# A table of offsets on the priorities of a planned order (attention and a gated feed-forward block, one core)

## The chip, the core and the metric

The kernel runs on one core of a Trainium2 chip, as one program. Its time is the device time of an execution in microseconds; 0.2% of it is about 1.5 us. Before the change three executions took 748.99, 749.52 and 750.12 us. The core has five engines that work side by side, each through its own list of instructions in the order in which they stand there: TensorE (PE, with its weight loads as PEld), VectorE (DVE), ScalarE (ACT), GpSimd (POOL) and SyncE (SP), which issues the DMAs.

## The reference

Eight batch elements of 576 tokens, eight heads of 64 columns each, in fp32. The output of the attention is the input of the feed-forward block:

```python
scores = scale * np.matmul(q, k.transpose(0, 1, 3, 2))
cum = np.cumsum(np.maximum(s, 0.0), axis=-1)
bias = -(cum[:, :, :, None] - cum[:, :, None, :])
scores = np.where(causal, -1e9, scores + np.minimum(bias, 0.0))
attn = np.exp(scores - np.max(scores, axis=-1, keepdims=True))
attn = attn / (np.sum(attn, axis=-1, keepdims=True) + 1e-09)
x = heads_side_by_side(np.matmul(attn, v))            # 8 x 576 x 512
h = gelu_tanh(x @ w_in)                               # 512 -> 1024
u, v = h[..., :512], h[..., 512:]
v_n = (v - mean(v)) / np.sqrt(var(v) + 1e-6) * g_ln
v_s = np.einsum('ts,bsd->btd', w_sg, v_n) + b_sg[None, :, None]
return x + (u * v_s) @ w_out
```

## The kernel before, in words

The 64 pairs of batch element and head are called heads 0 to 63 here. For each head the scores are made in four products of up to 512 columns, in two PSUM banks in turn (pss). VectorE adds the mask and takes the row minimum (the scores are negated) while it copies them out (`p<-pss,mask`, with `mn`); ScalarE takes the exponential and its sum; GpSimd multiplies by the reciprocal of the sum in seven pieces (`p<-p,rs`); TensorE transposes the result in twelve blocks (`psp<-ident,p`); ScalarE and VectorE copy the transposes to SBUF (`pT<-psp`); and every second head TensorE multiplies the transposes of a pair of heads by their values (`psp<-pT,vf`), which gives 128 of the 512 columns of the block's input (`xr`). Heads 0 to 7 use fp32 products. From head 8 on, numbers are split into two parts of reduced precision ("hi" and "lo"): ScalarE or GpSimd makes hi, GpSimd the rest (`k<-raw,k`, `xs<-xr,xs`).

The feed-forward block of a batch element needs the split input of its four pairs of heads (xs). It is cut into units, each one PSUM bank (psm, three in turn): v-units 0 to 4 (128 tokens by 512 columns; gelu, then mean and variance on VectorE, six small steps `rt` on GpSimd, then the normalized value is split into `vn`), u-units (288 columns, gelu), s-units (the product with the spatial weights ws, times u, split into `gt`) and o-units (the product with w_out, plus x, stored). The order of the units is a list in the source (`ORDER`; `ORD0` for the first element). A unit's bank is free for a later unit when VectorE or ScalarE have read it for the last time.

At the start, heads 0 to 7 are made while the weights come in: eight parts of w_in and four of w_out are unpacked from 64 bit floats by ScalarE and VectorE (`psm<-pair`, `gt<-pair,psm`) and split by ScalarE and GpSimd (`wi<-gt`, `wo<-gt`), and the spatial weights are split too (`ws<-u`). Later elements overlap: while the block of one runs, the heads of the next are made.

What sets the order: the function that builds the kernel does not issue instructions, it records them as operations with their dependences (class `Plan`; all then have the line of `issue`, L293 before the change). `Plan.order` gives every operation a cost from a table in the source, and goes forward through the plan, at each moment giving an engine the available operation with the lowest priority number; then backward, to get for each operation the time by which it has to start, which is its priority in the next round. After five rounds the last forward pass is the order that `issue` writes out on every engine:

```python
        prio = list(range(len(ops)))
        rounds = ROUNDS if rounds is None else rounds
        for i in range(rounds):
            res = self.forward(lat, prio)
            if i < rounds - 1:
                prio = self.backward(lat, [t + o.busy for t, o in zip(self.start, ops)])
        if SHIFT:
            shift = np.frombuffer(zlib.decompress(base64.b85decode(SHIFT)), np.int8)
            res = self.forward(lat, [p + 200.0 * float(x) for p, x in zip(prio, shift)])
        return res
```

Before the change `SHIFT` is None and the last block is skipped.

Of the kernel before, what the change touches and what calls it, by code (L numbers as in the profile page):

```python
# [20 lines left out]
B, H, S, D = 8, 8, 576, 64  # L21
BH = B * H
DM, DFF = 512, 1024
DH = DFF // 2
P = 128
NC = DM // P
# [16 lines left out]
PO = [0, 64, 256, 640, 1152]  # L43
# [18 lines left out]
PROBE = None  # L62
ROUNDS = 5

SHIFT = None
N3 = 8
XR = 10
G = 2
# [23 lines left out]
class Plan:  # L92
# [73 lines left out]
    def order(self, lat=LAT, rounds=None):  # L166
# [13 lines left out]
# [7 lines that stand above are left out]
# [921 lines left out]
```

## Time and profile before

| | before |
|---|---|
| median of three executions | 749.52 us |
| the profiled execution, and its span | 749.63 us, 747.9 us |
| busy: PE, PEld | 728.8, 634.5 us |
| busy: POOL, ACT, DVE | 542.8, 473.3, 472.4 us |
| mean granted clock of TensorE | 0.991 |
| DMA queue of the loads and stores | 85.85 MB, 41.7% of 16 engines |

The span is the time from the first to the last instruction of the profiled execution; the execution's own time has 1.7 us around it. Busy time of TensorE is the union of its matmuls, whose ends are modelled. [...] A wait is idle time of an engine, put down to what ended it.

### The profile page before, as it was taken

Reading aid. Unit: us, or ns where it says so; the run is one execution under the profiler, and the core shown is the slowest. Engines: PE = TensorE matmul, PEld = TensorE weight load, DVE = VectorE, ACT = ScalarE, POOL = GpSimd, SP = SyncE. Lnnn points to the kernel's source line nnn. Section 1 sums busy time; section 2 is a strip of 40 time slices with the busy share of each in tenths; the row PEclk is TensorE's granted clock in tenths of the full one; section 3 lists DMA queues with packets and bytes.
Section 4 is the critical chain, followed back from the end, with each engine's and each line's share of the span. In section 5 each row is a group of like instructions: output and inputs, shape, how many; then the busy total and the mean of one; then the engine's idle time right before and its main releaser. Section 6 shows DMA issues by size and latency. Waiting matters only on the chain.

```text
span 747.9 us, 15982 instructions
## 1 busy us (share of the span) xinstructions
PE 728.8 (97%) x5219; PEld 634.5 (85%) x5219; DVE 472.4 (63%) x1470; ACT 473.3 (63%) x1279; POOL 542.8 (73%) x978
## 2 busy tenths in 40 slices
PE   8899889999999999999999999999999999999998
PEld 5666678988889898998889888899888988998998
DVE  7997668447664676646685376745766466843752
ACT  4898778457675677646785476755776457842440
POOL 4799999768679487866878676795868768674541
PEclk9999889999999999999999999999999999999999
DMA  6777544245444254343543543443543434300101
GB/s 215 211 224 185 150 113 125 86 110 139 117 125 121 77 160 121 94 133 99 148 125 86 143 123 112 125 109 90 155 123 88 141 98 133 82 8 32 47 8 64
DMA packets 59239, 86.87 MB, mean 116 GB/s; under 512 B 16482, under 2 KB 34148, under 8 KB 59156
## 3 DMA queue, kind: packets, MB, share of 16 engines
q1 hardware_dynamic: 59156, 85.85, 41.7%
q8 instruction: 41, 0.67, 0.4%
q14 instruction: 42, 0.34, 0.2%
HBM read 39.89 MB, written 9.73 MB: 66 GB/s over the span
## 4 chain that ended last, share of the span: by engine, by line
PE 87%; DVE 6%; POOL 2%; DMA 2%; issue 1%; ACT 1%; SPq 1%; POOLq 0%; DVEq 0%
PE psm L293 53%; PE psp L293 20%; PE pss L293 13%; DVE p L293 2%; DVE psm L293 2%; DMA pair<-in_w_in 1%; POOL p L293 1%; POOL xs L293 1%; DVE u L293 1%; POOL k L293 1%; SPq L293 1%; DVE gt L293 0%; DVE vt L293 0%; DMA k<-xs 0%; DVE pT L293 0%
## 5 line engine op out<-in xcount | busy, mean ns | idle before, releaser
L293 POOL TENSOR_SCALAR p<-p,rs 128x448 f32<-128x448 f32 x434 | 192.5, 452 | 26.0 <-DVE rs L293 8.9
L293 ACT ACTIVATE p<-p,mn 128x448 f32<-128x448 f32 x310 | 171.8, 556 | 49.6 <-DVE mn L293 49.2
L293 DVE CUSTOM_DVE_ANT_0 p<-pss,mask 128x448 f32<-128x448 f32 x310 | 122.0, 422 | 63.9 <-PE pss L293 55.1
L293 PE MATMUL pss<-k,q 128*128 128x288 f32 (+10 forms) x768 | 148.2, 311 | 6.2 <-DVE mn L293 5.7
L293 PEld LDWEIGHTS pss<-k,q 128*128 128x128 f32 (+3 forms) x768 | 120.7, 184 | 24.1 <-DVE mn L293 9.0
L293 PE MATMUL psm<-xs,wi 128*128 128x288 f32 x720 | 114.7, 303 | 2.8 <-DVE u L293 2.3
L293 PE MATMUL psm<-gt,wo 128*128 128x288 f32 x720 | 117.1, 301 | 0.0
L293 PE MATMUL psm<-ws,vn 128*128 128x288 f32 x708 | 112.3, 297 | 0.0
L293 PE MATMUL psm<-wi,xs 128*128 128x512 f32 (+1 forms) x380 | 105.5, 405 | 1.2 <-DVE vt L293 0.8
L293 PEld LDWEIGHTS psm<-xs,wi 128*128 128x128 f32 x720 | 100.6, 191 | 5.5 <-DVE u L293 3.7
L293 PEld LDWEIGHTS psm<-gt,wo 128*128 128x128 f32 x720 | 101.1, 188 | 1.9
L293 POOL TENSOR_TENSOR k<-raw,k 128x576 fp32r<-128x576 f32 x56 | 79.7, 1424 | 29.7 <-ACT k L293 28.5
L293 PEld LDWEIGHTS psm<-ws,vn 128*128 128x128 f32 x708 | 99.3, 188 | 0.4
L293 PE MATMUL psp<-pT,vf 128*64 128x64 f32 (+4 forms) x768 | 94.1, 393 | 0.2 <-ACT pT L293 0.2
L293 POOL TENSOR_TENSOR gt<-u,gt 128x288 fp32r<-128x288 f32 (+1 forms) x66 | 52.8, 804 | 51.4 <-ACT gt L293 51.4
L293 PEld LDWEIGHTS psp<-pT,vf 128*64 128x64 f32 x768 | 47.6, 137 | 49.0 <-issue 35.4
L293 ACT COPY pT<-psp 128x512 f32<-128x512 f32 x128 | 70.4, 579 | 20.0 <-PE psp L293 18.8
L293 PEld LDWEIGHTS psm<-wi,xs 128*128 128x128 f32 (+1 forms) x380 | 67.3, 187 | 14.8 <-DVE vt L293 1.1
L293 PEld LDWEIGHTS psp<-ident,p 128*128 128x128 f32 x744 | 69.7, 141 | 6.0 <-POOL p L293 4.2
L293 PE MATMUL psp<-ident,p 128*128 128x128 f32 x744 | 72.1, 248 | 2.8 <-POOL p L293 2.8
L293 ACT CAST gt<-u 128x288 fp32r<-128x288 f32 (+1 forms) x66 | 28.1, 429 | 61.8 <-DVE u L293 59.3
L293 DVE SCALAR_TENSOR_TENSOR u<-u,psm 128x288 f32<-128x288 f32 x120 | 52.4, 444 | 13.5 <-ACT u L293 12.4
(124 smaller groups left out, 1040.2 us busy)
## 6 DMA issues: line engine op xcount, KB each, us to landing
q<-k SPq DMA_DIRECT2D x168, 144.0 KB
raw<-in_kq SPq DMA_DIRECT2D x56, 288.0 KB
vf<-in_vp SPq DMA_DIRECT2D x64, 192.0 KB
out_t<-u SPq DMA_DIRECT2D x64, 144.0 KB
k<-k SPq DMA_DIRECT2D x56, 144.0 KB
pair<-in_w_in SPq DMA_DIRECT2D x8, 512.0 KB
pair<-in_w_out SPq DMA_DIRECT2D x4, 512.0 KB
u<-xs SPq DMA_DIRECT2D x32, 64.0 KB
```

The lines of the kernel that those rows point to most:

```text
L293: fn(*args, **kw)
```

## The change

One constant of the source changes; the code that reads it was there before, and all other lines stay:

```diff
-SHIFT = None
+SHIFT = (
+    'c-mc<^;;C*AND1rJ48YnDQOXrMoN$nkP!R`h)A=*0`n)Fh3$n68g}XKmhNt(yCkGR1fKQzUe7Pj>zA2pu9<7jobx{S`@UyKx)Fd<E@i$yPbjB6MY;Lf+1G'
+    '!rdkc2^d>(>?l!9;E{e(KUXJ>lt%_OwU4`p}@4fv15e_J-{+{duoU5RM~PrbOF(}c{#Mf|3&z8u7AF$KrfG%;~?_2mp^^dI!wH0S)Ba9?wq9xD@{>{sQm`'
...
+)
```

Unpacked, the text is 6,828 whole numbers from -120 to 120, one for each recorded operation; all but 18 are not zero. 200 times its number is added to an operation's priority, up to 24,000 of the plan's nanoseconds either way, and one more forward pass makes the order from these priorities. Operations, tiles and buffers are as before, so names agree between the two; the lines of the recorded instructions are 71 further down (L364). All five engines' lists come out in another order. TensorE's has 2,553 rows of equal neighbours before and 2,667 now. Three places follow, all between the first heads and the start of the first feed-forward block.

GpSimd, where the split of the fourth pair's input (xs_97, from heads 6 and 7) is made. Before; rs_92 is head 8's normalization, k2_117 the key split of head 11, ws_4 the spatial weights:

```order
L293 TENSOR_TENSOR ws_4_70<-u2_120_189,ws_4_70 128x288
L293 TENSOR_SCALAR p_0_66<-p_0_66,rs_92_161 128x448
L293 TENSOR_SCALAR p_0_66<-p_0_66,rs_92_161 64x64
L293 TENSOR_SCALAR p_0_66<-p_0_66,rs_92_161 128x320
L293 TENSOR_SCALAR p_0_66<-p_0_66,rs_92_161 128x128
L293 TENSOR_SCALAR p_0_66<-p_0_66,rs_92_161 64x64
L293 TENSOR_SCALAR p_0_66<-p_0_66,rs_92_161 128x512
L293 TENSOR_SCALAR p_0_66<-p_0_66,rs_92_161 64x64
L293 TENSOR_TENSOR ws_4_70<-u2_127_196,ws_4_70 128x288
L293 TENSOR_SCALAR xs_97_166<-xr_93_162 128x576
L293 TENSOR_TENSOR k2_117_186<-raw_110_179,k1_116_185 128x576
L293 TENSOR_TENSOR xs_97_166<-xr_93_162,xs_97_166 128x576
```

Now:

```order
L364 TENSOR_TENSOR k2_100_169<-raw_91_160,k1_99_168 128x576
L364 TENSOR_SCALAR p_0_66<-p_0_66,rs_92_161 128x448
L364 TENSOR_SCALAR p_0_66<-p_0_66,rs_92_161 128x320
L364 TENSOR_SCALAR p_0_66<-p_0_66,rs_92_161 64x64
L364 TENSOR_SCALAR xs_97_166<-xr_93_162 128x576
L364 TENSOR_TENSOR ws_4_70<-u2_127_196,ws_4_70 128x288
L364 TENSOR_TENSOR xs_97_166<-xr_93_162,xs_97_166 128x576
L364 TENSOR_TENSOR wr2_33_102<-u2_139_208,wr1_32_101 64x288
L364 TENSOR_TENSOR ws_4_70<-u2_114_183,ws_4_70 128x288
L364 TENSOR_TENSOR ws_4_70<-u2_115_184,ws_4_70 128x288
L364 TENSOR_SCALAR p_0_66<-p_0_66,rs_92_161 128x512
L364 TENSOR_SCALAR p_0_66<-p_0_66,rs_92_161 64x64
```

Four pieces of head 8's normalization, the key split and two splits of spatial weights (the two had been in front of the first row shown) now stand behind the second instruction of xs_97.

TensorE, at the transposes of head 9 (ident, p_3) and the start of v-unit 3 (psm1 from xs_79, xs_82, xs_90 and xs_97). Before; k1_116 is the key of head 11:

```order
L293 MATMUL psp2_62<-ident_16_85,p_3_69 128x128 x4
L293 MATMUL psp0_60<-ident_16_85,p_3_69 128x128 x4
L293 MATMUL psp1_61<-ident_16_85,p_3_69 128x128 x4
L293 MATMUL pss0_58<-k1_116_185,q1_118_187 128x448
L293 MATMUL pss0_58<-k2_117_186,q2_1_27_96 128x448
L293 MATMUL pss0_58<-k1_116_185,q1_118_187 64x64
L293 MATMUL pss0_58<-k2_117_186,q2_1_27_96 64x64
L293 MATMUL pss1_59<-k1_116_185,q1_118_187 128x320
L293 MATMUL pss1_59<-k2_117_186,q2_1_27_96 128x320
L293 MATMUL pss1_59<-k1_116_185,q1_118_187 128x192
L293 MATMUL pss1_59<-k2_117_186,q2_1_27_96 128x192
L293 MATMUL psm1_64<-wi_30_99,xs_79_148 128x512 x3
```

Now; k1_99 is the key of head 10, and u2_157 begins v-unit 4:

```order
L364 MATMUL psm0_63<-wi_30_99,xs_97_166 128x512
L364 MATMUL psm1_64<-wi_30_99,xs_79_148 128x512 x3
L364 MATMUL psm1_64<-wi_30_99,xs_82_151 128x512 x3
L364 MATMUL psm1_64<-wi_30_99,xs_90_159 128x512 x3
L364 MATMUL pss1_59<-k1_99_168,q1_101_170 128x288
L364 MATMUL pss1_59<-k2_100_169,q2_0_25_94 128x288
L364 MATMUL psm1_64<-wi_30_99,xs_97_166 128x512 x2
L364 MATMUL pss0_58<-k1_99_168,q1_101_170 128x288
L364 MATMUL pss0_58<-k2_100_169,q2_0_25_94 128x288
L364 MATMUL psm1_64<-wi_30_99,xs_97_166 128x512
L364 MATMUL psm2_65<-wi_30_99,u2_157_226 128x512
L364 MATMUL psp2_62<-ident_16_85,p_3_69 128x128 x4
```

All twelve matmuls of v-unit 3 and the first of v-unit 4 now stand ahead of the transposes of head 9; before, the transposes and the first scores of head 11 stood ahead of v-unit 3.

VectorE, around the reductions of v-unit 0 (vt_122 in bank psm1, bs_123, mv_124). Before; rs_111 is head 9's reciprocal, mn_119 head 10's scores, vt_134 and bs_135 are v-unit 1:

```order
L293 RECIPROCAL rs_111_180<-rs_111_180 128x5
L293 ISA p_0_66,mn_119_188<-pss0_58,mask_17_86 128x448
...
L293 ISA p_0_66,mn_119_188<-pss0_58,mask2_18_87 128x288
...
L293 SCALAR_TENSOR_TENSOR vt_122_191<-vt_122_191,psm1_64 128x512
L293 SCALAR_TENSOR_TENSOR vt_134_203<-vt_134_203,psm2_65 128x512
L293 ISA p_0_66,mn_119_188<-pss1_59,mask2_18_87,mn_119_188 128x288
...
L293 SCALAR_TENSOR_TENSOR psm1_64<-vt_122_191,psm1_64 128x512
L293 SCALAR_TENSOR_TENSOR psm2_65<-vt_134_203,psm2_65 128x512
L293 BN_STATS bs_123_192<-psm1_64 128x6
L293 BN_STATS bs_135_204<-psm2_65 128x6
L293 BN_AGGR mv_124_193<-bs_123_192 128x2
...
L293 SCALAR_TENSOR_TENSOR vt_122_191<-psm1_64,mv_124_193,g_b_20_89 128x512
```

Now; mn_104 is head 9's scores:

```order
L364 ISA p_2_68,mn_104_173<-pss0_58,mask2_18_87 128x288
...
L364 SCALAR_TENSOR_TENSOR vt_122_191<-vt_122_191,psm1_64 128x512
L364 ISA p_2_68,mn_104_173<-pss1_59,mask2_18_87,mn_104_173 128x288
...
L364 SCALAR_TENSOR_TENSOR psm1_64<-vt_122_191,psm1_64 128x512
L364 BN_STATS bs_123_192<-psm1_64 128x6
L364 SCALAR_TENSOR_TENSOR vt_134_203<-vt_134_203,psm2_65 128x512
L364 BN_AGGR mv_124_193<-bs_123_192 128x2
L364 RECIPROCAL rs_111_180<-rs_111_180 128x5
L364 SCALAR_TENSOR_TENSOR vt_122_191<-psm1_64,mv_124_193,g_b_20_89 128x512
L364 ISA p_0_66,mn_119_188<-pss0_58,mask_17_86 128x448
```

V-unit 0 gets its mean and variance (BN_AGGR) ahead of the reciprocal of head 9 and of all of head 10's scores, which stood ahead of it or between its steps.

## Rows read from the trace of the kernel before

**Rows 1.** The page's part 1: busy time, share of the span and instructions of each engine.

```profile
PE 728.8 (97%) x5219; PEld 634.5 (85%) x5219; DVE 472.4 (63%) x1470; ACT 473.3 (63%) x1279; POOL 542.8 (73%) x978
```

**Rows 2.** Windows: us, busy us of PE, PEld, DVE, ACT, POOL; PEclk, DMA share, GB/s.

```profile
10.00:62.00 52.00, 46.41 (x272) 31.50 (x271) 49.75 (x154) 45.85 (x133) 40.37 (x66) 1.00 0.73 220
62.00:80.00 18.00, 16.72 (x106) 12.32 (x107) 10.51 (x39) 13.60 (x38) 17.12 (x26) 1.00 0.69 163
80.00:104.00 24.00, 18.94 (x102) 14.15 (x101) 15.40 (x52) 18.66 (x51) 22.58 (x45) 0.80 0.51 136
104.00:145.00 41.00, 41.00 (x314) 37.45 (x314) 27.63 (x91) 29.72 (x83) 37.87 (x65) 0.95 0.41 111
145.00:640.00 495.00, 493.30 (x3656) 435.95 (x3655) 307.75 (x987) 319.42 (x868) 367.91 (x667) 1.00 0.44 119
720.00:748.00 28.00, 24.62 (x186) 24.38 (x184) 8.21 (x19) 3.84 (x10) 6.28 (x8) 1.00 0.14 48
```

**Rows 3.** Windows of the two stretches at a lower granted clock.

```profile
84.30:91.20 6.90, 6.05 (x20) 4.80 (x17) 4.65 (x17) 4.42 (x16) 6.90 (x15) 0.51 0.67 182
101.40:108.30 6.90, 6.03 (x28) 5.49 (x29) 5.67 (x17) 4.48 (x12) 6.44 (x16) 0.51 0.38 98
```

**Rows 4.** Waits of TensorE: us in total, times, longest.

```profile
PE pss L293 <- DVE mn L293: 5.7, 8, 1.5
...
PE psp L293 <- POOL p L293: 2.8, 2, 1.8
...
PE psm L293 <- DVE u L293: 2.3, 6, 0.6
...
PE pss L293 <- DMA k<-cum: 0.4, 1, 0.4
```

**Rows 5.** Timeline of TensorE from 70 to 110 us: start, length, instructions, idle before.

```profile
76.32 1.66 PE L293 MATMUL psm<-wi,xs 128*128 128x512 f32 x6 [0.18 <-POOL xs L293]
...
82.81 1.23 PE L293 MATMUL psp<-ident,p 128*128 128x128 f32 x12 [1.81 <-POOL p L293]
...
86.65 3.78 PE L293 MATMUL psm<-wi,xs 128*128 128x512 f32 x8 [0.85 <-DVE vt L293]
...
100.50 0.53 PE L293 MATMUL pss<-k,q 128*128 128x288 f32 x2 [1.16 <-DVE mn L293]
...
101.78 0.85 PE L293 MATMUL pss<-k,q 128*128 128x288 f32 x2 [0.75 <-DVE mn L293]
...
103.11 3.25 PE L293 MATMUL psm<-xs,wi 128*128 128x288 f32 x12 [0.48 <-DVE vt L293]
```

**Rows 6.** Groups of GpSimd's instructions by shape: count, busy us, mean ns.

```profile
L293 POOL TENSOR_TENSOR k<-raw,k 128x576 fp32r<-128x576 f32 x56 | 79.7, 1424 | 29.7 <-ACT k L293 28.5 <-DVE mn L293 1.2
...
L293 POOL TENSOR_SCALAR p<-p,rs 64x64 f32<-64x64 f32 x186 | 58.4, 314 | 10.3
...
L293 POOL TENSOR_SCALAR p<-p,rs 128x512 f32<-128x512 f32 x62 | 42.9, 693 | 5.4
...
L293 POOL TENSOR_SCALAR p<-p,rs 128x128 f32<-128x128 f32 x62 | 22.6, 365 | 0.0
...
L293 POOL TENSOR_TENSOR rt<-rt 128x1 f32<-128x1 f32 x96 | 18.4, 192 | 5.1
...
L293 POOL TENSOR_TENSOR rt<-rt,half 128x1 f32<-128x1 f32 x32 | 18.1, 565 | 1.9
...
L293 POOL TENSOR_TENSOR ws<-u,ws 128x288 fp32r<-128x288 f32 x8 | 6.3, 800 | 0.0
```

**Rows 7.** Timeline of GpSimd from 66 to 84 us.

```profile
77.97 1.42 POOL L293 TENSOR_TENSOR xs<-xr,xs 128x576 fp32r<-128x576 f32 x1
...
79.37 3.38 POOL L293 TENSOR_SCALAR p<-p,rs 128x448 f32<-128x448 f32 x7
```

**Rows 8.** Timeline of TensorE in two batches: the wait that recurs.

```profile
211.08 1.86 PE L293 MATMUL psm<-xs,wi 128*128 128x288 f32 x12 [0.43 <-DVE u L293]
...
298.67 1.58 PE L293 MATMUL psm<-xs,wi 128*128 128x288 f32 x10 [0.32 <-DVE u L293]
```

69 lines of the change are left out of this document (added).

## The prediction

> **What bounds the kernel now.** I read the busy times first. TensorE is busy for 97% of the span, the others for 63 to 73% [rows 1], so an order can only save what TensorE loses. The stretches say where that is [rows 2]: idle is 5.59 us from 10 to 62, 1.28 from 62 to 80, 5.06 from 80 to 104, nothing to 145, 1.70 in the 495 us from 145 to 640, and 3.38 in the last 28, of 19.1 in all (747.9 less 728.8 [rows 1]). The regular part, over 60% of the time, loses 0.3%: the question is settled in the first 104 us. There the cover is the other way round: from 10 to 62 VectorE is busy for 49.75 of 52 us, from 62 to 104 GpSimd for 39.7 of 42.
>
> [...]
>
> The waits themselves come last [rows 4, 5]. At 82.81 the transposes of head 9 wait for GpSimd's normalization; at 86.65 v-unit 3 waits for the bank that v-unit 0 holds until VectorE has read it; at 100.50 and 101.78 the scores of head 12 wait for the reductions that free their banks; at 103.11 u-unit 0 waits for the bank of v-unit 2.
>
> **The change part by part.** Nothing is removed or added: equal instructions, equal durations. TensorE's list goes from 2,553 to 2,667 rows of equal neighbours, so units are interleaved more finely; each instruction keeps its cost. I sum the moves by stretch.
>
> First, the fourth pair's split on GpSimd. It ends at 79.39 [rows 7] and all v-units need it. Seven instructions that stood ahead of it now stand behind: two splits of the spatial weights (0.80 each), one key split (1.42), and the last four pieces of head 8's normalization (0.69, 0.37 and twice 0.31), together 1.60 + 1.42 + 1.68 = 4.7 us [rows 6]. GpSimd has next to no idle time there, so work ahead is time: the split could end near 74.7. VectorE must not lose this lead again: v-unit 0's reductions now stand ahead of head 10's scores and of head 9's reciprocal, where before they stood behind and among them.
>
> Second, what pays for it. Ahead of the big piece of head 9's normalization now stand two splits of 0.80 and v-unit 0's six small steps (one power 0.57, five of about 0.19 [rows 6]): 1.60 + 0.57 + 0.95 = 3.1 us later, from 82.75 [rows 7] to about 86. TensorE's transposes of that head are behind v-unit 3 now, whose twelve matmuls fill up to 12 x 1.66/6 = 3.3 us [rows 5]. So the wait for head 9 is covered by the unit that waited for a bank before, if that bank comes as early as the first step says.
>
> The gain of the two together is at least 4.7 - 3.1 = 1.6 us, lead less lag, and at most the idle time of 80 to 104, 5.1 us. A loss is left to the rival below. I take 3.0, nearer the lower end, since head 9's normalization is what TensorE may still wait for.
>
> Third, the clock. Its two ends are a gain of 6.0 (both slow stretches gone) and a loss of 3.0 (a third one, if waits fall together elsewhere). With roughly half of the idle time gone I take one stretch gone: 3.0.
>
> Fourth, 10 to 62 us. The steps that unpack the weights (eight for the input, four for the output matrix) go behind score reductions on VectorE. VectorE's idle time there is 2.25 us, so the gain is at most that; a loss of the same size could come from unpacked weights that are late. I take 0: nearly all of these steps stay in that stretch. SP's moves belong here: the first weight load now goes out behind two others, and the key loads come up to a few places later or earlier. The nearest price is the one wait of TensorE for a DMA, 0.4 us [rows 4], and behind each of these loads stand other loads; I take 0, with 0.4 as the end on either side.
>
> Fifth, 145 to 640. The order is different in every round, but TensorE's work is the same. The gain is at most the 1.70 us of idle time; the loss has no bound but the second rival's. I take 0: engines other than TensorE have idle time of a quarter (GpSimd 368 of 495) to a third, which hides a move of some us. If that cover fails, each uncovered wait costs its 0.4 to 0.7 us (2.3 over 6 and 5.7 over 8 [rows 4]).
>
> Sixth, the end. The last 3.38 us are mostly the last addition and store, which nothing in the order shortens; the closing output units are still matmuls alone. 0.
>
> Sum: 3.0 + 3.0 = 6.0 us. The profiled execution took 749.63 us (747.9 of span and 1.7 around it), 0.1 over the median 749.52; 749.6 - 6.0 is 743.6.
>
> [...] From 145 to 640 the idle time is 1.70 us and the granted clock 1.00 throughout [rows 2]; short waits there cost nothing more. [...]
>
> **Rivals.** (a) More goes than I take: all idle time from 62 to 104 and both slow stretches: 749.6 - 6.3 - 6.0 = 737.3, and with the 1.7 of the regular part 735.6. For it speaks that the waits lie on one chain (split, v-unit, bank, next unit); against it that head 9 comes later.
>
> (b) Slower: new waits in the regular part. Each engine works its list in order. Where GpSimd or VectorE now reaches an instruction whose input isn't there, everything behind it is held, the next head's pieces too, and TensorE, with three banks for the units, has nothing else. The part has 495/87.6 = 5.65 rounds of eight heads (one batch of the input takes 298.67 - 211.08 = 87.6 us, from one wait for VectorE to its like [rows 8]). Two waits of 0.71 us a round are 8.0 us; if the clock falls in two of the rounds, 6.0 more. 749.6 - 6.0 + 8.0 + 6.0 = 757.6. It decides from about 1.1 us of new waits a round, against 0.30 now (1.70/5.65). Against it: GpSimd and VectorE have a quarter or more to spare; for it: the finer interleaving, and GpSimd's norm pieces with statistics steps between them. [...]
>
> (c) No change: head 9's pieces now stand alternately with v-unit 0's statistics steps on GpSimd. If VectorE delivers the statistics late, GpSimd stands and the lead of 4.7 is spent there: idle moves from the bank to the transposes, the clock falls as before. 749.6 - 0 = 749.6.
>
> That the table does nothing is excluded: all five engines' lists differ.
>
> **How the numbers follow.** The forecast, 737 to 748, gets 0.58, with 743.6 as its time; rival (a), under 737, 0.13; (c) 0.11; (b) 0.18. 0.2% is 1.5 us, about what a measurement of this kernel can tell from no change. Faster is the forecast and (a), 0.71; same is (c), 0.11; slower is (b), 0.18. The range leaves out a tenth at either end: 734 (1.6 under (a) with all) to 753, in the midst of (b). It is wide because one term, the clock, comes in steps of 3 us and the regular part has no upper bound.
>
> **What would show it.** Step one: the fourth pair's split ends 4 to 5 us earlier, v-unit 3 starts near 82 instead of 86.65. Step two: the transposes of head 9 wait less than 1.8 us, or not at all, behind v-unit 3. Step three: one stretch of half clock in the first 110 us instead of two. Step five: idle time of TensorE under 3 us from 145 to 640 and the clock at 1.00. The prediction is wrong if the idle time of 62 to 104 stays at 6.3, if both slow stretches stay, or if the regular part loses more than 7 us.

## The result

The time goes from 749.25 us (746.32 to 750.12) to 741.05 us (740.72 to 741.86), four executions each, a ratio of 0.9899 with a 95% interval of 0.9870 to 0.9927. A second comparison, with 15 executions of before, gave 741.09 and 0.9893 (0.9874 to 0.9912). The profiled execution of after took 741.86 us, its span is 740.1 (747.9 before): 7.8 us less.

Busy time of after, from the page's part 1 [rows 1]: TensorE has 6.0 us less, the others nearly the same.

```profile
PE 722.8 (98%) x5219; PEld 632.5 (85%) x5219; DVE 470.3 (64%) x1470; ACT 479.1 (65%) x1279; POOL 543.6 (73%) x978
```

Windows of after [rows 2]; the columns are those of before, and the last window ends 0.1 us ahead of the span's end:

```profile
10.00:62.00 52.00, 46.56 (x272) 31.45 (x270) 46.66 (x151) 44.69 (x129) 39.95 (x67) 1.00 0.73 209
62.00:80.00 18.00, 16.69 (x93) 12.88 (x94) 12.67 (x39) 14.79 (x39) 16.57 (x25) 0.91 0.64 177
80.00:104.00 24.00, 20.24 (x144) 16.11 (x143) 17.73 (x60) 20.68 (x57) 23.36 (x49) 1.00 0.55 143
104.00:145.00 41.00, 40.19 (x320) 36.05 (x319) 28.43 (x91) 31.23 (x86) 40.09 (x66) 1.00 0.47 122
145.00:640.00 495.00, 495.00 (x3678) 440.14 (x3677) 309.34 (x1001) 328.39 (x882) 370.91 (x672) 1.00 0.45 120
640.00:720.00 80.00, 80.00 (x577) 74.03 (x576) 43.28 (x101) 33.79 (x80) 42.86 (x81) 1.00 0.07 22
720.00:740.00 20.00, 16.91 (x128) 16.68 (x126) 6.13 (x14) 2.48 (x6) 3.96 (x5) 1.00 0.17 60
```

The same for the one window of before that was not shown:

```profile
640.00:720.00 80.00, 79.41 (x568) 72.48 (x567) 47.10 (x118) 39.48 (x96) 44.83 (x87) 1.00 0.10 30
```

TensorE's idle time from 62 to 104 us went from 6.34 to 5.07 us only, while it got through more: 144 matmuls instead of 102 from 80 to 104, at a granted clock of 1.00 instead of 0.80. From 145 to 720 us there is no idle time left, and 3,678 + 577 = 4,255 matmuls stand in the same 575 us that held 3,656 + 568 = 4,224: 31 more (22 by 640 us, 9 behind it), at 575/4,255 = 0.135 us each an estimated 4.2 us (3.0 and 1.2).

The granted clock, which the profile gives as a share of full speed: both half-clock stretches of before [rows 3] are gone, in the same windows it is 1.00. One of half the length is new, from 62.9 to 66.3 us:

```profile
62.90:66.30 3.40, 3.40 (x14) 2.71 (x13) 3.31 (x12) 3.27 (x11) 3.22 (x6) 0.50 0.90 243
84.30:91.20 6.90, 6.21 (x39) 4.28 (x39) 5.22 (x20) 6.30 (x19) 6.90 (x15) 1.00 0.53 135
101.40:108.30 6.90, 5.49 (x42) 5.13 (x43) 5.33 (x19) 5.79 (x15) 6.72 (x14) 1.00 0.42 100
```

TensorE's waits in after [rows 4]: the six for VectorE's u steps in the regular part are gone (the one here is at 102 us), those for VectorE's reductions fell from 5.7 to 1.2 us, and DMA waits rose from 0.4 to 3.2.

```profile
PE psm L364 <- DVE u L364: 2.0, 1, 2.0
PE pss L364 <- DMA k<-in_kq: 1.7, 1, 1.7
PE pss L364 <- DMA k<-cum: 1.5, 1, 1.5
...
PE pss L364 <- DVE mn L364: 1.2, 3, 0.5
```

TensorE's timeline of after [rows 5], then GpSimd's [rows 7]; of the latter the rows at 72.83 and 74.25 are the fourth pair's split, the last is the last large piece of head 9's normalization:

```profile
62.58 1.74 PE L364 MATMUL pss<-k,q 66*128 66x320 f32 x7 [1.50 <-DMA k<-cum]
...
82.00 2.56 PE L364 MATMUL psm<-wi,xs 128*128 128x512 f32 x10
...
86.87 1.22 PE L364 MATMUL psp<-ident,p 128*128 128x128 f32 x12
...
95.50 1.22 PE L364 MATMUL psp<-ident,p 128*128 128x128 f32 x12 [1.07 <-POOL p L364]
...
102.00 1.86 PE L364 MATMUL psm<-xs,wi 128*128 128x288 f32 x12 [2.00 <-DVE u L364]
```

```profile
69.66 1.42 POOL L364 TENSOR_TENSOR k<-raw,k 128x576 fp32r<-128x576 f32 x1 [0.64 <-ACT k L364]
71.42 1.44 POOL L364 TENSOR_SCALAR p<-p,rs 128x448 f32<-128x448 f32 x3 [0.35 <-DVE rs L364]
72.83 0.67 POOL L364 TENSOR_SCALAR xs<-xr 128x576 fp32r<-128x576 f32 x1
...
74.25 1.43 POOL L364 TENSOR_TENSOR xs<-xr,xs 128x576 fp32r<-128x576 f32 x1
...
85.64 0.69 POOL L364 TENSOR_SCALAR p<-p,rs 128x512 f32<-128x512 f32 x1
```

**Lead at equal work.** The order differs, so equal times do not stand at equal places. To compare, each matmul is counted with the median time from its start to the next one's start for its form, over before and after beyond 115 us; that makes 686.9 us of work in both. The time at which a kernel has done a given amount is read from its trace. Grouping the forms otherwise moves the readings at 35 to 60 us of work by up to 2 us, those from 80 on by about 0.1. Ahead of before (minus: behind) after is by:

| work done, us | before at | after at | lead |
|---|---|---|---|
| 35 | 56.14 | 56.95 | -0.8 |
| 40 | 62.98 | 66.68 | -3.7 |
| 55 | 83.13 | 83.13 | 0.0 |
| 60 | 92.17 | 89.29 | +2.9 |
| 80 | 118.67 | 115.09 | +3.6 |
| 180 | 222.37 | 218.41 | +4.0 |
| 400 | 449.38 | 443.96 | +5.4 |
| 686.9 | 744.62 | 736.91 | +7.7 |

So in this pair of executions about half of the gain, 3.6 us, is there at 118 us, and the other half, 4.1 us, comes little by little behind it, about 3 us by 640 us and 1 us after that.

### The profile page after: what moved, and what is told of

Same layout as the page of the kernel before. It is cut to its first block, busy times and chain, and to the rows that moved or that the text cites. A ratio compares the mean times of both kernels' runs of the same rounds, so it can differ in the third digit from the quotient of the medians.

```text
span 740.1 us, 15928 instructions
## 1 busy us (share of the span) xinstructions
PE 722.8 (98%) x5219; PEld 632.5 (85%) x5219; DVE 470.3 (64%) x1470; ACT 479.1 (65%) x1279; POOL 543.6 (73%) x978
## 4 chain that ended last, share of the span: by engine, by line
PE 88%; POOL 3%; DMA 3%; DVE 2%; ACT 1%; SPq 1%; issue 1%; ACTq 0%; POOLq 0%; DVEq 0%
PE psm L364 54%; PE psp L364 20%; PE pss L364 14%; DMA vf<-in_vp 1%; SPq L364 1%; DMA pair<-in_w_in 1%; POOL p L364 1%; POOL k L364 1%; DVE psm L364 1%; DVE p L364 1%; DMA raw<-in_kq 1%; POOL vn L364 0%; POOL ws L364 0%; DMA q<-k 0%; POOL rt L364 0%
## 5 line engine op out<-in xcount | busy, mean ns | idle before, releaser
L364 POOL TENSOR_SCALAR p<-p,rs 128x448 f32<-128x448 f32 (+4 forms) x434 | 193.6, 455 | 32.0 <-DVE rs L364 17.6
L364 ACT ACTIVATE p<-p,mn 128x448 f32<-128x448 f32 (+3 forms) x310 | 172.4, 558 | 47.0 <-DVE mn L364 44.8
L364 DVE CUSTOM_DVE_ANT_0 p<-pss,mask 128x448 f32<-128x448 f32 (+3 forms) x310 | 122.5, 421 | 56.1 <-PE pss L364 39.9
L364 PE MATMUL pss<-k,q 66*128 66x288 f32 (+10 forms) x768 | 149.1, 313 | 4.6 <-DMA k<-in_kq 1.7
L364 PEld LDWEIGHTS pss<-k,q 128*128 128x128 f32 (+3 forms) x768 | 118.8, 183 | 22.5 <-DVE mn L364 6.7
L364 PE MATMUL psm<-gt,wo 128*128 128x288 f32 x720 | 122.2, 298 | 0.0
L364 PE MATMUL psm<-xs,wi 128*128 128x288 f32 x720 | 117.3, 299 | 2.5 <-DVE u L364 2.0
L364 PE MATMUL psm<-ws,vn 128*128 128x288 f32 x708 | 116.8, 298 | 0.0
L364 PE MATMUL psm<-wi,xs 128*128 128x512 f32 (+1 forms) x380 | 106.0, 401 | 0.6 <-DVE gt L364 0.6
L364 PEld LDWEIGHTS psm<-gt,wo 128*128 128x128 f32 x720 | 104.5, 188 | 2.3 <-POOL gt L364 0.2
L364 PEld LDWEIGHTS psm<-xs,wi 128*128 128x128 f32 x720 | 102.0, 188 | 4.3 <-DVE u L364 2.2
L364 PEld LDWEIGHTS psm<-ws,vn 128*128 128x128 f32 x708 | 101.0, 188 | 1.1
L364 POOL TENSOR_TENSOR k<-raw,k 128x576 fp32r<-128x576 f32 x56 | 79.9, 1427 | 24.0 <-ACT k L364 20.7
L364 PE MATMUL psp<-pT,vf 128*64 128x64 f32 (+4 forms) x768 | 94.1, 393 | 1.0 <-ACT pT L364 1.0
L364 POOL TENSOR_TENSOR gt<-u,gt 128x288 fp32r<-128x288 f32 (+1 forms) x66 | 52.8, 806 | 56.4 <-ACT gt L364 55.9
L364 ACT COPY pT<-psp 128x512 f32<-128x512 f32 x128 | 71.2, 581 | 27.3 <-PE psp L364 26.3
L364 PEld LDWEIGHTS psp<-pT,vf 128*64 128x64 f32 x768 | 47.6, 137 | 48.1 <-issue 34.5
L364 PEld LDWEIGHTS psm<-wi,xs 128*128 128x128 f32 (+1 forms) x380 | 67.1, 185 | 12.9 <-DVE gt L364 0.7
L364 PE MATMUL psp<-ident,p 128*128 128x128 f32 x744 | 71.9, 247 | 1.9 <-POOL p L364 1.4
L364 PEld LDWEIGHTS psp<-ident,p 128*128 128x128 f32 x744 | 69.7, 141 | 4.5 <-POOL p L364 2.3
L364 ACT CAST gt<-u 128x288 fp32r<-128x288 f32 (+1 forms) x66 | 28.1, 429 | 59.4 <-DVE u L364 48.3
L364 DVE SCALAR_TENSOR_TENSOR u<-u,psm 128x288 f32<-128x288 f32 x120 | 52.6, 445 | 18.5 <-ACT u L364 17.9
```

What stands on the lines that cost most here:

```text
L364: fn(*args, **kw)
```

## The experiments

Theory A: the two halves are separate, the first from the places that the prediction names, the second from the regular part's own order. Theory B: one causes the other. Theory C: from 62 to 145 us GpSimd, not TensorE, sets the pace. The table has all kernels, with the median, the ratio to before beside it, and two readings at equal work: when 80 us of work are done (the end of the first part), and how long the last 506.9 us take, from 180 on.

| kernel | us | ratio (95%) | 80 us done at | from 180 to the end |
|---|---|---|---|---|
| before | 749.3 | | 118.67 | 522.25 |
| after | 741.05 | 0.9899 (0.9870 to 0.9927) | 115.09 | 518.50 |
| again | 741.09 | 0.9893 (0.9874 to 0.9912) | 114.26 | 518.52 |
| first | 749.94 | 1.0010 (0.9996 to 1.0025) | 115.77 | 522.23 |
| rest | 772.80 | 1.0316 (1.0292 to 1.0341) | 117.21 | 536.32 |
| from61 | 757.69 | 1.0113 (1.0092 to 1.0134) | 124.88 | 518.85 |
| bthena | 753.42 | 1.0064 (1.0044 to 1.0085) | 119.21 | 518.52 |
| cum | 744.06 | 0.9935 (0.9912 to 0.9957) | 120.29 | 518.65 |
| kq | 741.59 | 0.9898 (0.9877 to 0.9920) | 115.17 | 518.49 |
| undo | 743.71 | 0.9932 (0.9917 to 0.9948) | 115.68 | 518.65 |
| twice | 751.94 | 1.0043 (1.0024 to 1.0061) | 122.34 | 522.23 |
| swap | 747.99 | 0.9991 (0.9978 to 1.0005) | 115.11 | 522.06 |
| swap2 | 747.58 | 0.9983 (0.9964 to 1.0002) | 115.26 | 521.58 |
| fill | 748.28 | 0.9998 (0.9984 to 1.0012) | extra work | extra work |

The two readings come from one profiled execution each. The last column hardly differs between executions: 522.25, 522.23 and 522.23 in before, first and twice, 518.50 and 518.52 in after and again. The column ahead of it does: swap and swap2, whose lists are before's on every engine up to 116 us, have 115.11 and 115.26 where before has 118.67. Their profiled executions (745.38 and 745.31 us) are among the fastest of theirs (medians 747.99 and 747.58). So a lead at 80 us of work in one pair of executions does not show by itself what an order gains. By the medians after gains 8.2 us, of which 3.7 lie behind 180 us of work and some 4.5 ahead of it.

**Parts of the table** (first, rest, from61). The offsets act by the time at which the plan without them starts an operation:

```diff
-  [p + 200.0 * float(x) for p, x in zip(prio, shift)]
+  [p + 200.0 * float(x) * (t < 115000.0) for p, x, t in zip(prio, shift, list(self.start))]   # first
+  ... (t >= 115000.0) ...   # rest
+  ... (t >= 61000.0) ...    # from61
```

> The offsets act only on operations that the plan without offsets starts before 115 us; all later ones keep their priority. Theory A, separate parts: from the trace of after, the lead of TensorE over before at equal work is -3.7 us at 63 us, +3.6 at 118 us and +7.7 at 700 us; the part up to 118 us is worth 3.6 by itself, the time is 749.3 - 3.6 = 745.7 (745 to 746.7), and the six waits for VectorE's u steps in the regular part (0.3 to 0.6 us each) come back. Rival B, one cause: the regular part runs without waits because it is entered with a lead; then this kernel takes about 741.1 and the six waits are gone.

> The offsets act only on operations that the plan without offsets starts at 115 us or later. Theory A: the first 115 us are those of before, both half-clock stretches stay, the six waits of the regular part are gone, and the time is 749.3 - 4.1 = 745.2 (744.2 to 746). Rival B: no gain without the lead of the first part: 748.5 to 749.5. A third way, that parts of the late table only fit a plan that is shifted as a whole, would show new waits after 118 us and more than 749.5.

> The offsets act only on operations that the plan without offsets starts at 61 us or later, so the loads and the unpacking of the first 61 us are as before. Theory A: the loss of 3.7 us that after has by 63 us (waits for a key load of 1.7 us and for a bias load of 1.5 us, and the half-clock stretch behind it) is not there, the gains of 7.3 (62 to 118 us) and 4.1 (later) stay: 749.3 - 11.4 = 737.9 (736.5 to 739). Rival: the loss of the early part is made up later anyway, since TensorE waits for GpSimd and VectorE from 62 to 104 us whatever it did before: 741 (740.5 to 742).

No time fits theory A or B; rest goes the third way named there. Not one part of the table gives its part of the gain, and two make the kernel slower than before. In first, TensorE has its lead at 118 us in the profiled execution (115.77 against 118.67) and loses it where the list goes over to before's order, the largest part at a normalization that GpSimd has not finished:

```profile
120.66 1.22 PE L364 MATMUL psp<-ident,p 128*128 128x128 f32 x12 [1.78 <-POOL p L364]
...
123.87 0.66 PE L364 MATMUL psm<-xs,wi 128*128 128x288 f32 x3 [0.74 <-DVE u L364]
```

In from61 the joint is worse:

```profile
83.31 0.85 PE L364 MATMUL pss<-k,q 128*128 128x288 f32 x2 [3.43 <-DVE mn L364]
...
96.28 1.74 PE L364 MATMUL psp<-ident,p 128*128 128x128 f32 x12 [3.47 <-POOL p L364]
```

and in rest there are such waits far behind the joint too, with half-clock stretches behind them (TensorE's timeline, then windows):

```profile
324.58 0.44 PE L364 MATMUL pss<-k,q 128*128 128x448 f32 x1 [3.05 <-ACT k L364]
```

```profile
205.70:209.10 3.40, 3.40 (x14) 2.43 (x15) 3.26 (x9) 3.37 (x10) 3.32 (x4) 0.50 0.15 33
...
325.20:332.00 6.80, 6.30 (x25) 5.83 (x26) 2.17 (x4) 0.44 (x2) 5.08 (x10) 0.50 0.58 136
```

The reason is in how the plan is made: priorities are only compared among operations that are available at a moment. With another beginning other operations are available, and the same offsets make another order. In the middle of TensorE's list (from 40 to 50% of it) only 48% of the rows of rest stand as in after, 100% in from61. And there the table's last column tells: from61 enters the regular part 15 us later than after, and from then on takes 518.85 us for what after does in 518.50 and before in 522.25. First, with before's order there, takes 522.23. So the second half of the gain belongs to the order of the regular part alone; theory B falls, and of theory A the separation stands, not its sums, which left out the joint.

**Two orders joined** (bthena): operations that before's plan starts before 150 us in its order, the others in the order of after.

```diff
+  one, two, t = base, alt, at   # before's order, after's order, before's planned times
+  head = [k for k in one if t[k] < 150000.0]
+  done = set(head)
+  res = head + [k for k in two if k not in done]
```

> The order of before for all operations that its plan starts before 150 us, and behind them the rest in the order of after. Theory A: from 180 us to the end the order of after took 518.5 us in after, 518.7 and 518.9 in the two kernels that reach it 5 and 15 us later, against 522.2 of before; the gain of the regular part does not need the first: 749.3 - 3.7 = 745.6 (744.8 to 746.5) if the seam costs nothing. Rival B: the two parts belong together and the seam costs what the part gains: 748.5 or more.

The time, 753.42, lies in rival B's "748.5 or more", and the seam does cost more than the part gains. But the part's own gain is there without the first part (518.52), which is theory A's half of it; that the two parts belong together does not follow. The joint alone costs 9 us between 140 and 180 us, at two waits and a half-clock stretch:

```profile
158.00 0.53 PE L369 MATMUL pss<-k,q 128*128 128x288 f32 x2 [1.58 <-DVE mn L369]
161.54 1.25 PE L369 MATMUL pss<-k,q 128*128 128x448 f32 x4 [3.00 <-DMA k<-k]
```

```profile
160.30:167.10 6.80, 5.56 (x18) 2.49 (x20) 0.00 (x0) 0.00 (x0) 0.26 (x1) 0.50 0.05 16
```

**Step one undone** (undo): six instructions put back in front of the fourth pair's split.

```diff
+  ...
+  late = pool[n + 1:n + 8]      # what follows the split on GpSimd
+  at = res.index(xs[0])
+  move = [k for k in late if all(res.index(d) < at or d in late for d in ops[k].deps)]
+  for k in move:
+      res.remove(k)
+  res[at:at] = move
```

> After, with step one undone on GpSimd: six instructions that stand behind the split of the fourth pair's input there (two splits of the spatial weights, the last four pieces of head 8's normalization, 1.57 + 1.74 = 3.3 us in after's trace) are put in front of it, as before the change; the split ends near 78.9 instead of 75.6 us. Theory A: all v-units wait for it, TensorE loses 3.3 us less what it can do in between: 743 to 744.5, and 745 to 746 if a half-clock stretch comes back. Rival C: GpSimd's work up to 145 us is the same in sum, so the order in it matters little: 741 to 741.6.

743.71, and 0.9932 beside again's 0.9893, whose interval it does not meet: 2.9 us lost (2.6 by the medians). It does overlap the wider interval of the first comparison (to 0.9927), but the quickest of undo's six executions, 742.87 us, is slower than the slowest of the eight of after and again, 742.00. The wait is where step one has it. GpSimd's split and TensorE's first matmuls from it in undo:

```profile
74.81 0.67 POOL L377 TENSOR_SCALAR xs<-xr 128x576 fp32r<-128x576 f32 x1
...
76.22 1.42 POOL L377 TENSOR_TENSOR xs<-xr,xs 128x576 fp32r<-128x576 f32 x1
```

```profile
75.54 0.95 PE L377 MATMUL psm<-wi,xs 128*128 128x512 f32 x3 [2.52 <-POOL xs L377]
```

The first instruction of the split ends at 75.48, and TensorE goes on at 75.54 after 2.52 us; in after it ended at 73.50 and there was no wait. The whole split ends at 77.64 instead of 75.68: 3.3 us of work ahead of it make it 2.0 us later, since GpSimd's waits of 0.64 and 0.35 us in after are gone here. Theory A's 743 to 744.5 holds; theory C in the form that the order on GpSimd does not matter falls.

**More work for GpSimd** (twice): three splits executed twice, on before.

```diff
-  for fn, args, kw in self.ops[k].calls:
+  for fn, args, kw in self.ops[k].calls * (2 if k in again else 1):
```

> Before, with three splits of the spatial weights on GpSimd (0.80 us each, at 67 to 69.3 us) executed twice, 2.4 us of work more and nothing else. Theory C: from 62 to 145 us GpSimd is the bound (in six kernels TensorE's lead at 145 us goes with the GpSimd work done by then): 749.3 + 2.4 = 751.7 (751 to 754, more if another half-clock stretch comes). Rival, TensorE is the bound there and GpSimd has spare time: 749.3 to 749.8.

Plus 3.2 us (1.8 to 4.6) for 2.4 us of work: GpSimd has no spare time at 67 to 69 us, the one place tried. TensorE's waits in it, for head 8's pieces (none in before) and for the bank behind v-unit 0 (0.85 in before [rows 5]):

```profile
77.00 1.23 PE L297 MATMUL psp<-ident,p 128*128 128x128 f32 x12 [2.35 <-POOL p L297]
...
89.75 2.50 PE L297 MATMUL psm<-wi,xs 128*128 128x512 f32 x5 [2.83 <-DVE vt L297]
```

Together with undo this speaks for GpSimd as the bound of the first part: its work in sum, and the order of what TensorE needs from it.

**The clock** (fill): six matmuls of no use in the wait before head 9's transposes, on before.

```diff
+  if k == self.mark:
+      for _ in range(6):
+          self.nc.tensor.matmul(self.bank, self.left, self.right, start=True, stop=True)
```

> Before, with six 512-column matmuls of no use put on TensorE in front of the transposes of head 9, into the bank that these overwrite: they fill the wait of 1.81 us at 82.8 us (six took 1.66). Nothing else of the order changes. Theory A (step three): the wait is what lets the clock fall; the half-clock stretch that begins at 84.3 us (6.83 us) is gone and all of its 3.0 us come off: 749.3 - 3.0 = 746.3. Theory B: the stretch goes, but from 80 to 104 us TensorE waits for GpSimd, and the time that it would save is waited: 748.5 to 749.3. Over 17 executions of before the time falls by 480 us per unit of mean clock, which would make 2.2 us of the 6.83 us at half: 747.1, between the two. Rival: the clock falls for another reason and stays as it was: 749.3 or a little more.

The wait of 1.81 shrank to 0.40, the next one grew from 0.85 to 1.42, and the half-clock stretch that follows lasts 3.4 us in the profiled execution, 6.83 in that of before:

```profile
80.25 1.55 PE L294 MATMUL psp<-wi,ident 128*128 128x512 f32 x6
82.20 1.23 PE L296 MATMUL psp<-ident,p 128*128 128x128 f32 x12 [0.40 <-POOL p L296]
...
86.02 3.64 PE L296 MATMUL psm<-wi,xs 128*128 128x512 f32 x8 [1.42 <-DVE vt L296]
```

```profile
85.95:89.35 3.40, 3.33 (x8) 2.69 (x9) 2.23 (x11) 2.18 (x9) 3.40 (x8) 0.50 0.70 170
```

The mean granted clock over its executions is 0.9939, over those of before beside it 0.9923; the time is the same (0.9998). That fits theory B of this run and excludes theory A's 3.0 us, but it does not show that time given back was waited for again: by the slope below 0.0016 of mean clock goes with 0.7 us, less than the interval (0.9984 to 1.0012) can tell. Nor does it show that the wait of 1.81 us brings the stretch. Swap and swap2 (below), whose lists up to here are before's, wait 1.74 and 1.77 us in the same place and 1.47 and 1.43 at the next, and their clock is 1.00 from 84.3 to 91.2; the half-clock stretch comes at 97.3. TensorE in swap, then two windows of it:

```profile
81.22 1.22 PE L316 MATMUL psp<-ident,p 128*128 128x128 f32 x12 [1.74 <-POOL p L316]
...
85.06 2.13 PE L316 MATMUL psm<-wi,xs 128*128 128x512 f32 x8 [1.47 <-DVE vt L316]
```

```profile
84.30:91.20 6.90, 6.14 (x39) 4.13 (x40) 3.91 (x17) 4.99 (x17) 6.81 (x19) 1.00 0.57 143
97.30:104.10 6.80, 5.79 (x23) 4.90 (x23) 5.91 (x18) 4.92 (x16) 6.53 (x15) 0.50 0.53 131
```

So where the clock falls differs between executions of one order, and the shorter stretch in fill may be no more than that. Over 68 executions of before the time falls by 461 us per unit of mean clock (correlation -0.86), about 1.05 us for 3.41 us at half the clock, but an execution with longer waits may have both, and fill did not part them.

**SP's queue** (cum, kq, again). In after TensorE waits 1.50 us for the bias row of head 8 and 1.72 for head 4's key.

```diff
+  res.insert(i, res.pop(j))   # cum: 512 KB of output weights behind the bias load
```

```diff
+  new = sorted(run, key=rank)   # kq: of a head's three loads key, query, bias row in this order
+  ...
+  for p, x in zip(at, new):
+      res[p] = x
```

> After with one move on SP's queue: the load of 512 KB of output weights that is issued 0.44 us ahead of the bias load of head 8 is issued behind it. Theory A: the wait of 1.5 us at 62.6 us goes, and with it the one stretch at half the clock (3.41 us, worth 1.7): 741.05 - 3.2 = 737.9 (737 to 739). Rival 1: the wait goes but the half-clock stretch stays or comes elsewhere: 739.5. Rival 2: the bias load is late for another reason (queues full of other loads) and the wait stays: 741.

> After, with the three loads of a head (key, query, bias row) issued on SP's queue in before's order, the key first, for the four of heads 2 to 7 where the table has another order. Theory A: the wait of 1.7 us for head 4's key at 30.7 us goes, since the key is issued 1.2 us earlier, and a lead that TensorE has at 62 us stays: 741.2 - 1.2 = 740 (739.3 to 740.7). Rival: up to 62 us VectorE is the bound (46.7 of 52 us busy) and the lead is spent there, or from 62 us on for GpSimd: 741.2, as the run of after beside it.

> After once more, unchanged, on the chip of the two runs beside it, so that they and the kernels derived from it are compared with it and not with another chip's times. All theories: ratio to before 0.990 (0.988 to 0.992), about 741.5.

Cum was missed by all: slower than after by 3 us. The wait at the bias row is gone; in the profiled execution the weights that now come later are late for ScalarE, which holds its copies of pT behind them, and TensorE waits for these. ScalarE in after and in cum, and TensorE in cum:

```profile
62.33 0.63 ACT L364 ACTIVATE psm<-pair 128x512 f32<-128x512 f32 x1 [1.20 <-DMA pair<-in_w_out]
```

```profile
66.25 0.63 ACT L367 ACTIVATE psm<-pair 128x512 f32<-128x512 f32 x1 [2.44 <-DMA pair<-in_w_out]
```

```profile
63.39 1.25 PE L367 MATMUL pss<-k,q 128*128 128x320 f32 x8
...
68.37 1.19 PE L367 MATMUL psp<-ident,p 128*128 128x128 f32 x12 [2.72 <-ACT pT L367]
```

That is not all of it. This execution (746.95 us) is the slowest of cum's six, and it is 2.7 us behind after's already ahead of the moved load: the bias load is issued at 60.48 instead of 57.81, behind a wait of 2.11 us for ScalarE's pT at 42.14 (0.47 in after), when ScalarE had waited 1.54 us for a load of input weights that the move does not touch. How much of the 3 us the move costs by itself is not told apart.

In kq a wait of 1.5 us stayed (1.72 in after, 1.47 in again) and only its name changed, from the key to the bias row: the product needs all three loads, and TensorE goes on at 30.75, where it did at 30.70 in after.

```profile
PE pss L387 <- DMA k<-xs: 1.5, 1, 1.5
```

In again, the same kernel as after, the wait for head 8's bias row does not occur at all, the half-clock stretch lies at 102 us instead of 63, and the time is the same. So these waits vary from one execution to the next. Whether what they cost is made up behind, where TensorE waits for GpSimd, is not shown: TensorE starts the same 24 products `psp<-pT,vf` at 67.76 in again and at 69.06 in after, 1.3 us apart, and 80 us of work are done at 114.26 and 115.09, still 0.8 apart. Why the three loads land late was not tried.

**The six waits of the regular part** (swap, swap2, on before): VectorE's step that frees a u-unit's bank goes ahead of v-unit 4's (swap), and the reduction that frees the score bank goes ahead of three more steps (swap2).

```diff
+  order.insert(i, order.pop(j))   # swap: the u step ahead of v-unit 4's second gelu step
+  order.insert(p, order.pop(q))   # swap2, besides: the reduction ahead of v-unit 4's statistics
```

> Before, with one move on VectorE in each batch: the last step of a u-unit's gelu, which frees the bank that the next u-unit on TensorE waits for, is put ahead of the second step of v-unit 4's gelu (64x512, 0.68 us), behind which it stands. Theory A (regular part): the gain of after from 180 us on, 3.7 us, is these waits; six of 0.32 to 0.59 us of idle time, each 0.14 to 0.16 longer from start to start, 3.3 us together: 748.9 - 3.3 = 745.6 (745 to 746.5). Rival 1: the wait comes back elsewhere in the batch, since v-unit 4's step is later: 748.5 to 749.3. Rival 2: the gain of after comes from its finer interleaving of units, of which these waits are a part: 747 to 748.

> The run before with one more move on VectorE in each batch: the reduction that frees the score bank for which TensorE now waits (0.30 us, once a batch) is put ahead of three steps that no one on TensorE waits for (v-unit 4's statistics 0.69, a u step 0.43, the aggregation 0.17). Theory A: VectorE is busy for 99% of 8 us there, but only the order in this burst holds TensorE; with both waits gone the stretch from 180 us to the end takes 519 (522.25 in before, 522.06 in the run with one move, 518.5 in after), and the time is 749.3 - 3.3 = 746 (745.2 to 746.8). Rival: the burst itself is the bound, whatever its order; the wait moves on once more: 521.5 to 522.3 and 748 to 749.4.

Theory A fell both times. The times alone decide little between the rivals (swap's 747.99 lies in rival 2's range, swap2's 747.58 below its rival's, and both intervals reach 1); the traces show the wait come back, as rival 1 of swap and the rival of swap2 have it. In swap the waits for the u bank are gone but for the last, and four times TensorE waits in the same place for the score bank instead (the row names ScalarE, whose event came at the same moment; the reduction that frees the bank ends on VectorE at 296.08):

```profile
296.19 0.74 PE L316 MATMUL pss<-k,q 128*128 128x448 f32 x4 [0.31 <-ACT k L316]
```

In swap2 that wait goes too. Idle time from 145 to 640 fell from 1.70 to 1.21 and 0.34 us (swap, swap2):

```profile
145.00:640.00 495.00, 493.79 (x3660) 436.77 (x3658) 310.17 (x994) 322.36 (x879) 367.83 (x668) 1.00 0.44 119
```

```profile
145.00:640.00 495.00, 494.66 (x3661) 437.34 (x3660) 310.32 (x994) 322.43 (x879) 368.10 (x668) 1.00 0.44 119
```

and yet the stretch from 180 us of work on fell from 522.25 to 522.06 and 521.58 only. In swap2 there is a wait of 0.06 to 0.07 us once a batch at the next unit, where 0.23 us are lost from start to start. Before and after in the stretch of 8 us in which this happens:

```profile
294.00:302.00 8.00, 7.68 (x62) 7.28 (x61) 7.54 (x27) 7.82 (x24) 7.43 (x13) 1.00 0.51 128
```

```profile
291.00:299.00 8.00, 8.00 (x67) 6.49 (x66) 7.25 (x25) 7.89 (x22) 5.46 (x11) 1.00 0.17 37
```

In before VectorE, ScalarE and GpSimd are all busy for 93 to 98% of these 8 us; both times the step that was put ahead made another one late. In after, at the same place of its batch, GpSimd is at 68%, VectorE at 91 and ScalarE at 99, and TensorE's 8 us are full. Counted from start to start, the 3.7 us from 180 us of work on are five of the six waits (four of 0.48 us and one of 0.76, 2.7 in all) and about ten fewer losses of 0.1 us at changes between units. In swap2 the waits that are left cost 4 x 0.23 + 0.50 = 1.4 of the 3.1 us that it takes longer than after; the rest are such small losses. What of the order of after avoids both, beyond that units stand more finely between each other, stays open.

## Why the prediction was right and where it was not

The forecast was 743.6 for 741.05, and its sum of 6.0 stands against 8.2. The two halves of the sum are not where it put them.

**First, the split.** It ends at 75.68 (74.25 + 1.43) instead of 79.39, 3.7 us earlier where 4.7 were counted: GpSimd now waits 0.64 and 0.35 us ahead of it, which the count of moved instructions had left out. V-unit 3 starts at 82.00 as said, with no wait. Undo shows the mechanism and its price, 2.6 to 2.9 us.

**Second, what pays.** Head 9's last large piece ends at 86.33 (about 86 predicted), its transposes run at 86.87 without a wait for GpSimd. But the size was off: I took 3.0 us, and idle time from 62 to 104 us fell by 1.3. Ahead of these transposes v-unit 4's first matmul waits 0.69 us for a bank (`vt`, at 86.50), and two new waits take most of the rest: 1.07 at 95.50, now for head 10's pieces, and 2.00 at 102.00, where two u-units follow each other in one bank.

**Third, the clock.** One stretch gone for 3.0 was taken; both went and half of one came at 62.9. The 3.0, which also stands behind the 6.0 us in rivals (a) and (b), was my estimate, half of the 6.05 us for which TensorE was busy at a granted clock of 0.51 [rows 3]; no run shows the term, and the clock does not come in steps of it: the stretch in after lasts 3.40 us, half as long as either of before. What the runs show in its place is a correlation: by the slope over executions the rise of the mean clock from 0.9912 to 0.998 goes with 3.1 us. That waits bring the stretch was not shown either: swap and swap2 have the waits of the first one (1.81 and 0.85 us in before [rows 5], 1.74 and 1.47 in swap, 1.77 and 1.43 in swap2), in the order of before, and a clock of 1.00 from 84.3 to 91.2. How much the clock does by itself is not shown.

**Fourth, the loads.** 0 with 0.4 as the end on either side: the profiled execution lost some 3.7 us against before by 63 us, at waits of 1.72 and 1.50 that no row of before has and in the half-clock stretch from 62.9 on. The end was too near, and the 0 was wrong with it. From there to 118 us after gains 7.3 us; whether a part of these is this loss made up is not shown. Steps one to four together gave 3.6 us in the profiled pair, some 4 by the medians, where the sum has 6.0.

**Fifth, the regular part: this step failed.** "The question is settled in the first 104 us" and "the gain is at most the 1.70 us of idle time" are both wrong: 4.1 us, half of the gain, came from 118 us on, about 3 of them by 640 us. Bthena shows that those behind 180 us of work need nothing of the first part. The bound counted idle time only. A wait listed with 0.43 or 0.32 us of idle time made the next matmul start 0.59 or 0.48 us later than its form does without one, the last of the six (0.59 idle) lay behind 640 us, and losses of about 0.1 us at changes between units (125 in before from 180 us of work on, 115 in after) have no idle time in the profile at all. Idle time here is counted to a matmul's modelled end; in swap2 0.07 us of it stand beside 0.23 us from start to start.

**Sixth, the end.** From TensorE's last matmul to the end of the span it is 3.28 us before and 3.19 now (the 3.38 counts 0.1 us of the window [rows 2] behind the span): 0, as said. The sum has no term for 640 to 720 us, where before has 0.59 us of idle time and about 1 us of the gain lies.

**The rivals.** Rival (b), new waits and a falling clock in the regular part, did not happen in after: its order is finer there, TensorE has no idle time from 145 to 640 us and the clock is 1.00. In rest, whose order there is neither before's nor after's, it did, 23 us in all: the clock fell at 205.7 behind waits of 0.98 and 0.43 us and at 325.2 behind one of 3.05 us. That an engine holds what stands behind an instruction whose input is late is seen in cum: ScalarE waits 2.44 us for weights, its copies of pT behind them start at 67.66, and TensorE waits 2.72 us for these.

So the time came out right by luck: in the profiled pair steps one to four were too large by 2.4 us (6.0 for 3.6), and the regular part was too small by 4.1 (0 for 4.1). The mechanism of step one was right, and of step two that TensorE would not wait for head 9; the source of half of the gain was not foreseen.

## What to carry to other kernels

Compare two orders at equal work, not at equal times, before saying where a gain comes from; a sum that comes out right does not show that its terms do. Where one batch after another is nearly full, look for the stretch in which several helpers are full at once: here one step put ahead passed most of the wait on, twice (from 180 us of work on 522.06 and 521.58 us for 522.25), and another order of the units took it away (518.50). Before a gain is given to a place in a profile, look at how far that place moves between executions of one order: here by 3.5 us. A table of offsets, found for one plan as a whole, may not be divisible: parts of it made this kernel up to 3% slower.

## What the runs showed of the hardware

- The time of one kernel went with its mean granted clock (correlation -0.86 over 68 executions, the cause of either not shown): executions of before at 0.995 took 746.6 us on average, those at 0.988 took 750.2. With six extra matmuls in one wait the time could not be told from before's (0.9984 to 1.0012).
- The same order, with waits of about 1.8 us and then 0.9 to 1.5 us in the same two places, had a granted clock of 0.51 behind them in one execution (before) and of 1.00 in two others (swap, swap2): eight 512-column matmuls took 3.78 us there in before and 2.13 us in swap.
- Loads issued at about the same times landed differently in two executions of one kernel: the bias row of head 8, issued 0.44 us behind 512 KB in both, was waited for 1.50 us in one, until 4.77 us after its issue, and not at all in the other, where its product started 3.60 us after the issue.
- An idle time of 0.06 to 0.07 us on TensorE, which lists of waits hardly show, cost 0.23 us from start to start.
